# Static attention scores by half tiles: 64 queries times the 192 columns they need

## The chip, the core and the metric

The kernel runs on one core of a Trainium2 chip. TensorE multiplies matrices, VectorE, ScalarE and GpSimd work elementwise, SyncE issues most of the DMA transfers. The metric is the device time of one execution in microseconds. A run takes it several times; the medians are compared.

## What is computed

Four batches of eight heads, 768 positions of 64 numbers each, float32 throughout. A block-sparse attention is followed by a feed-forward layer:

```python
scores = (1.0 / np.sqrt(D)) * np.matmul(q, k.transpose(0, 1, 3, 2))
blk_i, blk_j = pos[:, None] // 32, pos[None, :] // 32
mask = np.abs(blk_i - blk_j) <= 1
mask = mask | (blk_i == 0) | (blk_j == 0) | (blk_i == 23) | (blk_j == 23)
for qb in range(24):
    for kb in sampled_blocks[qb]:                       # 3 per block
        mask[qb * 32:(qb + 1) * 32, kb * 32:(kb + 1) * 32] = True
scores = np.where(mask, scores, -1000000000.0)
...
attn = np.exp(scores - np.max(scores, axis=-1, keepdims=True))
attn = attn / (np.sum(attn, axis=-1, keepdims=True) + 1e-09)
x = attn @ v                                            # then [3072, 512]
h = x @ w_in                                            # 512 x 2048
out = (s * np.maximum(h, 0.0) ** 2 + b) @ w_out         # 2048 x 512
```

So a block of 32 queries sees its own block and the two neighbours, the first and the last block, and three sampled ones. The first and the last block of queries see all keys.

## The kernel before

**Order.** Attention comes first (0 to about 280 us), then the feed-forward layer, whose weights come as float64 and are taken apart into a high and a low part (the decode, lines 75 to 85) by VectorE and ScalarE, partly during attention. From about 546 us on the last two batches go through a scheme with seven products in place of eight (L1193).

**Slots.** The 22 middle blocks of queries are shifted by one block, so that a tile t of 128 queries holds four whole blocks. A static slot ("s") is one batch b, one tile t of 0 to 4 and one half x of the heads: 4 x 5 x 2 = 40 slots, each of four units, a unit being 128 queries of one head. Besides there are 8 slots "d" (the two blocks that see everything, 384 columns and two parts) and 4 slots "h" (the last half tile). 

**One static slot on TensorE**, in this order:

1. `transposes` (L787): the weights of a unit, 128 queries by 352 columns, are turned in three pieces of 128x128 by a product with a unit matrix, four units, 12 records. They go to one bank of PSUM per unit.
2. `x_transpose` (L858): two more for the slot before.
3. `scores_static` (L710), for the slot two further on: 128 queries times 256 columns (the tile's own 128 keys, the 64 keys of first and last block, the 64 keys behind the tile). Its contraction is 64 long, so the two heads of a pair use the upper and the lower rows of the array at the same time (`tile_position=(par * D, 0)`); each writes to a bank of its own. Four products.
4. `scores_sampled` (L736): the 96 sampled columns, per block of 32 queries.
5. `av_static` (L832): the turned weights times the values, two chunks of 128 keys for each half of 64 queries, which use the left and the right columns of the array.
6. `av_sampled` (L846): the same for the 96 sampled keys, per block of 32 queries.

A float32 product is two records in the trace, a transposition one. The mode of the array that a product uses is its tile size: 128x128, 64x128, 64x64, 64x32, 128x64 or 128x32 rows by columns. It follows from the shape of the operands or is given.

**The other engines.** VectorE takes the maximum of a unit, adding the mask `ms` (L751); ScalarE the exponential (L763); both take turns in copying the turned weights out of PSUM (L791, L793). In `ms` of 352 columns lie the window mask (built at L568 to L573) and the mask of sampled columns. Eight buffers `ptile` hold the weights, seven banks of PSUM go round for scores and transpositions, an eighth holds the value products.

**What sets the order.** TensorE's order in attention is a fixed line: the transpositions of slot i, the output transpositions of slot i - 1, the scores of slot i + 2, the value products of slot i. For the other engines a planner (`Plan`) simulates the program as it is built, with costs in ns that stand in the code (L956, L993, L1000, L1005), and writes the instructions of each engine in the order that it finds. Loads of k, q and v, the gathers and the decode of the weights are placed by the same planner.

**Keys and values.** `k_seq` holds per tile of keys 128 columns and then the 64 of first and last block, so that the 256 columns that a tile needs stand together, from 192 t on. `v_sta` holds the values of these 256 keys as two chunks of 128 rows: chunk 0 the tile's own keys, chunk 1 first and last block (rows 0 to 63) and the 64 keys behind (rows 64 to 127).

Of the kernel before, what the change touches and what calls it, by code (L numbers as in the profile page):

```python
# [9 lines left out]
F32 = mybir.dt.float32  # L10
# [192 lines left out]
def kernel(  # L203
# [27 lines left out]
    SC = 256  # L231
# [227 lines left out]
    with ExitStack() as es:  # L459
# [95 lines left out]
        def sampled_blocks():  # L555
# [146 lines left out]
        def scores_static(i, k):  # L702
# [4 lines left out]
            if kind == "s":  # L707
                for par in range(2):
                    sp = sps[(n + 2 * k + par, 0)] = next_bank(f"s{n + 2 * k + par}")
                    nc.tensor.matmul(sp[:, :SC], qr[halves[par], 2 * x + k, :], kt[halves[par], 2 * x + k, 192 * t:192 * t + SC],  # L710
                                     start=True, stop=True, tile_position=(par * D, 0))
                return
# [69 lines left out]

        def transposes(n, g):
            src = pbuf[(n, g)]
            tp = tps[(n, g)] = next_bank(f"t{n}_{g}")[:, :3 * P].rearrange("p (c q) -> p c q", c=3)
            for c in range(chunks(n)):
                nc.tensor.transpose(tp[:, c, :], src[:, c * P:(c + 1) * P], ident)  # L787
# [24 lines left out]
        def av_static(i, j):  # L812
# [17 lines left out]
            for c in range(2):  # L830
                for rows in halves:
                    nc.tensor.matmul(xs[rows], pt[:, c, rows], vt[:, c, hp * D:(hp + 1) * D], start=(j == 0 and c == 0),  # L832
                                     stop=False, skip_group_check=True)

        def av_sampled(i):
            kind, b, t, x = slots[i]
            n, vg = unit_of[i], vgs[(b, t)]
            for j in range(4):
                xs, pt = out_of(i, j), pts_of.pop(n + j)[0]
                for r in range(4):  # L840
                    rows = slice(r * BLK, (r + 1) * BLK)
                    if kind == "s":
                        w, m, h = pt[:NSL * BLK, 2, rows], r, 4 * x + 2 * (j % 2) + j // 2
                    else:
                        w, m, h = pt[:, 0, rows], r % 2, 4 * x + 2 * j + r // 2
                    nc.tensor.matmul(xs[rows], w, vg[:w.shape[0], m, h * D:(h + 1) * D], start=False, stop=(j == 3),  # L846
                                     tile_position=(0, r * BLK), skip_group_check=True)
# [108 lines left out]
        costs = {"s": (485, 535, 350, 260, 685), "d": (810, 0, 350, 780, 0), "h": (380, 535, 240, 160, 685)}  # L956
        cols = {"s": (1024, 1536, 768, 256, 1024), "d": (1536, 0, 768, 768, 0), "h": (640, 768, 512, 128, 512)}
        for i, (kind, b, t, x) in enumerate(slots):
# [31 lines left out]
            for j in range(nu):  # L990
                n, ms_ = u + j, []
                for g in range(ng):
                    o_m = op("v", {"s": 600, "d": 680, "h": 500}[kind], n + T["MP"], lambda n=n, g=g: maximum(n, g),  # L993
# [4 lines left out]
                for g in range(ng):  # L998
                    top = g == 0 and j == 0
                    o_e = op("a", {"s": 780, "d": 800, "h": 700}[kind], n + T["EP"], lambda n=n, g=g: exp(n, g), ms_,  # L1000
# [4 lines left out]
                    o_ev = op(on, {"a": 380, "v": 430}[on] if kind == "h" else {"a": 490, "v": 560}[on], n + T["EV"], lambda n=n, g=g, e=on: evacuate(n, g, e),  # L1005
# [378 lines left out]
```

## Time and profile before

| | |
|---|---|
| median of 3 runs | 813.33 us (811.89 to 817.2) |
| the profiled execution | 810.37 us, of it the span from first to last instruction 808.6 |
| granted clock of TensorE, mean | 0.992 |
| busy: TensorE, VectorE, ScalarE, GpSimd | 784.5, 559.1, 494.0, 214.7 us |
| TensorE's lines with most time, share of the chain that ended last | L1193 13%, L441, L442 and L440 10% each, L787 8%, L832 5%, L710 5% |

The span is what the profile shows; the executions' times are slightly longer. The last row comes from the chain of work that ended last: followed back from the last instruction, at each step to what released it. TensorE has 84% of that chain. Matmuls are pipelined, and a record lasts longer than the time until the next one starts; so what a stage costs is read from start to start and not from the duration of its records.

### The profile page before, as it was taken

Reading aid. Unit: us, or ns where it says so; the run is one execution under the profiler, and the core shown is the slowest. Engines: PE = TensorE matmul, PEld = TensorE weight load, DVE = VectorE, ACT = ScalarE, POOL = GpSimd, SP = SyncE. Lnnn points to the kernel's source line nnn. Section 1 sums busy time; section 2 is a strip of 40 time slices with the busy share of each in tenths; the row PEclk is TensorE's granted clock in tenths of the full one; section 3 lists DMA queues with packets and bytes.
Section 4 is the critical chain, followed back from the end, with each engine's and each line's share of the span. In section 5 each row is a group of like instructions: output and inputs, shape, how many; then the busy total and the mean of one; then the engine's idle time right before and its main releaser. Section 6 shows DMA issues by size and latency. Waiting matters only on the chain.

```text
span 808.6 us, 21993 instructions
## 1 busy us (share of the span) xinstructions
PE 784.5 (97%) x8400; PEld 682.2 (84%) x8400; DVE 559.1 (69%) x1379; ACT 494.0 (61%) x1175; POOL 214.7 (27%) x438
## 2 busy tenths in 40 slices
PE   7899999999998999999999999999999999999997
PEld 6687877888886889999889999998889988899996
DVE  5576778888887899999742222288768869766662
ACT  3576777878787787777663333457445457544542
POOL 5422133222400032222322222223223223322321
PEclk9899999999999999999999999999999999999999
DMA  9999897887777532433221010412200012000002
GB/s 267 248 223 315 231 253 215 244 246 215 220 210 235 144 107 83 130 127 105 86 98 40 27 40 27 150 52 79 86 1 7 0 40 85 16 0 1 1 2 78
DMA packets 86073, 95.61 MB, mean 118 GB/s; under 512 B 11344, under 2 KB 64976, under 8 KB 85968
## 3 DMA queue, kind: packets, MB, share of 16 engines
q1 hardware_dynamic: 85968, 94.21, 39.0%
q8 instruction: 66, 1.08, 0.6%
q14 instruction: 39, 0.32, 0.1%
HBM read 77.41 MB, written 12.58 MB: 111 GB/s over the span
## 4 chain that ended last, share of the span: by engine, by line
PE 84%; DMA 4%; ACT 4%; DVE 3%; issue 3%; SPq 2%; POOL 0%; ACTq 0%; DVEq 0%; POOLq 0%
PE m L1193 13%; PE o L441 10%; PE o L442 10%; PE o L440 10%; PE t L787 8%; PE xs L832 5%; PE s L710 5%; PE h L402 5%; PE h L403 5%; PE h L401 5%; PE xs L846 3%; PE s L736 2%; DMA kt<-in_k_seq_dram 2%; PE s L724 1%; PE xs L821 1%
## 5 line engine op out<-in xcount | busy, mean ns | idle before, releaser
L419 POOL TENSOR_TENSOR hid<-hid,hid 128x384 fp32r<-128x384 f32 x128 | 139.4, 1090 | 438.9 <-ACT hid L415 255.8
L763 ACT ACTIVATE ptile<-ptile,nm 128x352 f32<-128x352 f32 (+2 forms) x208 | 120.8, 584 | 30.5 <-DVE nm L751 29.5
L1210 ACT ACTIVATE hid<-hid,sb_b,sb_s 128x384 f32<-128x384 f32 x64 | 45.3, 708 | 111.9 <-DVE hid L1204 111.8
L410 DVE SCALAR_TENSOR_TENSOR hid<-hid,sb_s 128x384 f32<-128x384 f32 x64 | 40.9, 641 | 89.0 <-ACT hid L406 88.9
L670 POOL COPY kg<-kt 128x128 f32 x264 | 63.6, 294 | 134.9 <-PE s L736 123.9
L751 DVE CUSTOM_DVE_ANT_0 ptile<-s,ms 128x352 f32<-128x352 f32 x160 | 74.3, 521 | 27.8 <-PE s L736 27.5
L401 PE MATMUL h<-x,win 128*128 128x384 f32 x256 | 86.6, 338 | 0.6 <-ACT hid L406 0.6
L402 PE MATMUL h<-x,win 128*128 128x384 f32 x256 | 86.2, 337 | 0.2 <-DVE x L374 0.2
L403 PE MATMUL h<-x,win 128*128 128x384 f32 x256 | 86.4, 337 | 0.0
L787 PE MATMUL t<-ident,ptile 128*128 128x128 f32 x608 | 79.6, 280 | 6.4 <-ACT ptile L763 3.5
L787 PEld LDWEIGHTS t<-ident,ptile 128*128 128x128 f32 x608 | 66.3, 142 | 12.4 <-ACT ptile L763 4.3
L442 PE MATMUL o<-wout,hid 128*128 128x512 f32 x192 | 76.0, 396 | 0.0
L442 PE MATMUL o<-woutr,hid 128*128 128x512 f32 x192 | 76.0, 396 | 0.0
L441 PE MATMUL o<-wout,hid 128*128 128x512 f32 x192 | 75.9, 395 | 0.0
L441 PE MATMUL o<-woutr,hid 128*128 128x512 f32 x192 | 75.8, 395 | 0.0
L440 PE MATMUL o<-wout,hid 128*128 128x512 f32 x192 | 74.8, 389 | 0.0
L440 PE MATMUL o<-woutr,hid 128*128 128x512 f32 x192 | 74.7, 389 | 0.0
L406 ACT ACTIVATE hid<-h 128x384 f32<-128x384 f32 x64 | 31.2, 487 | 54.3 <-PE h L403 52.4
L791 DVE COPY pt<-t 128x384 f32<-128x384 f32 (+1 forms) x104 | 56.1, 545 | 9.9 <-PE t L787 8.0
L414 ACT ACTIVATE hid<-hid,sb_b 128x384 f32<-128x384 f32 x64 | 39.4, 615 | 37.2 <-DVE hid L410 37.2
L1193 PE MATMUL m<-xT,wop 128*128 128x384 f32 x288 | 58.5, 337 | 2.6 <-DVE sum L1286 1.5
L793 ACT COPY pt<-t 128x384 f32<-128x384 f32 (+1 forms) x104 | 48.8, 473 | 15.7 <-PE t L787 14.9
(169 smaller groups left out, 1648.8 us busy)
## 6 DMA issues: line engine op xcount, KB each, us to landing
vg<-in_v_dram SPq DMA_DIRECT2D x136, 128.0 KB, 3.9
v<-in_v_sta_dram SPq DMA_DIRECT2D x40, 256.0 KB, 4.5
kt<-in_k_seq_dram SPq DMA_DIRECT2D x16, 544.0 KB, 8.2
raw_i<-in_w_in_dram SPq DMA_DIRECT2D x16, 512.0 KB, 4.9
raw_o<-in_w_out_dram SPq DMA_DIRECT2D x16, 512.0 KB, 3.2
v<-in_v_dram SPq DMA_DIRECT2D x16, 384.0 KB, 5.4
xd<-xst SPq DMA_DIRECT2D x44, 128.0 KB, 3.9
out_dram<-ob SPq DMA_DIRECT2D x20, 256.0 KB, 2.2
```

The source lines that it names most:

```text
L401: nc.tensor.matmul(ph, wh, xh, start=(c == 0), stop=False)
L402: nc.tensor.matmul(ph, wh, xl, start=False, stop=False)
L403: nc.tensor.matmul(ph, wl, xh, start=False, stop=(c == NCC - 1))
L419: nc.gpsimd.tensor_tensor(out=htile(5 + i % 3), in0=t, in1=gh.bitcast(F32), op=ALU.subtract)
L440: nc.tensor.matmul(acc, gh[:, tsl], wout(f, 0), start=first, stop=False)
L441: nc.tensor.matmul(acc, gh[:, tsl], wout(f, 1), start=False, stop=False)
L442: nc.tensor.matmul(acc, gl[:, tsl], wout(f, 0), start=False, stop=last)
L670: nc.gpsimd.tensor_copy(kg[:, m], kts[b][:, :, bass.ds(box["js"][m], BLK)])
L751: nc.vector.tensor_tensor_reduce(out=pt[:, :w], in0=sps.pop((n, g))[:, :w], in1=msk, scale=-scale, scalar=FMAX if g == 0 else nm[:, 0:1], ...
L763: nc.scalar.activation(pt[:, :w], pt[:, :w], AF.Exp, bias=nms[n][:, last:last + 1], scale=-1.0, accum_out=dns[i][:, g, j:j + 1])
L787: nc.tensor.transpose(tp[:, c, :], src[:, c * P:(c + 1) * P], ident)
L1193: nc.tensor.matmul(to, w_, x_, start=(c == 0 and k == 0), stop=(c == 1 and k == 2))
```

## The change

Of the 256 static columns each half of a tile needs 192. The first 64 queries see the tile's own 128 keys and the 64 of first and last block (which stand ahead of the tile in `k_seq`, or behind it for t = 0), the other 64 the tile's second half, first and last block, and the 64 keys behind. The change lets each half compute its own 192 columns, with 64x64 tiles of the array, four at a time. A unit becomes 288 columns wide in place of 352.

The turned weights then are two full pieces of 128x128, and one piece that differs between the halves: 64 columns each, turned by an ordinary product with a 64x64 part of the unit matrix. The value products take a full chunk of 128 keys for each half, and a second product of 64 keys for each half. In `k_seq`, `v_sta` and the number of DMA transfers nothing changes. The mask is built to the new places, and the planner's costs are lowered.

```diff
-    SC = 256
+
+    SA = 64
+    SC = 192
     SW = SC + NSL * BLK
...
-        nc.gpsimd.memset(ms[:, :, P:P + 2 * BLK], 0.0)
-        nc.scalar.copy(ms[:, :, :P].rearrange("p t (c e) -> p t c e", e=BLK),
-                       wm[:, :4].unsqueeze(1).unsqueeze(3).broadcast_to([P, NSP, 4, BLK]))
-        nc.scalar.copy(ms[:, :, P + 2 * BLK:SC].rearrange("p t (c e) -> p t c e", e=BLK),
-                       wm[:, 4:].unsqueeze(1).unsqueeze(3).broadcast_to([P, NSP, 2, BLK]))
-        nc.gpsimd.memset(ms[:, 0, :BLK], NEG)
+        def window(rows, to, c, n):
+            nc.scalar.copy(ms[rows, :, to:to + n * BLK].rearrange("p t (c e) -> p t c e", e=BLK),
+                           wm[rows, c:c + n].unsqueeze(1).unsqueeze(3).broadcast_to([D, NSP, n, BLK]))
+
+        nc.gpsimd.memset(ms[:D, :, :SA], 0.0)
+        window(slice(0, D), SA, 0, 4)
+        window(slice(D, P), 0, 2, 2)
+        nc.gpsimd.memset(ms[D:, :, SA:2 * SA], 0.0)
+        window(slice(D, P), 2 * SA, 4, 2)
+        nc.gpsimd.memset(ms[:D, 0, SA:SA + BLK], NEG)
...
             if kind == "s":
+
+
+                places = [(0, SA, 192 * t, P), (0, 0, 192 * t + P, SA)] if t == 0 else [(0, 0, 192 * t - SA, SC)]
                 for par in range(2):
-                    sp = sps[(n + 2 * k + par, 0)] = next_bank(f"s{n + 2 * k + par}")
-                    nc.tensor.matmul(sp[:, :SC], qr[halves[par], 2 * x + k, :], kt[halves[par], 2 * x + k, 192 * t:192 * t + SC],
-                                     start=True, stop=True, tile_position=(par * D, 0))
+                    sps[(n + 2 * k + par, 0)] = next_bank(f"s{n + 2 * k + par}")
+                for a, to, o, w in places + [(1, 0, 192 * t + SA, SC)]:
+                    for par in range(2):
+                        nc.tensor.matmul(sps[(n + 2 * k + par, 0)][halves[a], to:to + w], qr[halves[par], 2 * x + k, halves[a]],
+                                         kt[halves[par], 2 * x + k, o:o + w], start=True, stop=True, tile_position=(par * D, a * D))
                 return
...
+        def tcols(n):
+            return 2 * P + D if slots[units[n][0]][0] == "s" else chunks(n) * P
+
         def transposes(n, g):
             src = pbuf[(n, g)]
-            tp = tps[(n, g)] = next_bank(f"t{n}_{g}")[:, :3 * P].rearrange("p (c q) -> p c q", c=3)
+            tp = tps[(n, g)] = next_bank(f"t{n}_{g}")[:, :tcols(n)]
+            if slots[units[n][0]][0] == "s":
+
+                for c in range(2):
+                    nc.tensor.transpose(tp[:, c * P:(c + 1) * P], src[:, SA + c * P:SA + (c + 1) * P], ident)
+                for h in halves:
+                    nc.tensor.matmul(tp[h, 2 * P:], src[h, :SA], ident[h, h], start=True, stop=True)
+                return
...
         def evacuate(n, g, eng):
-            o = ptp.tile([P, 3, P], F32, tag="pt", name=f"pt{n}_{g}")[:, :chunks(n)]
-            pts_of.setdefault(n, []).append(o)
-            copy_on(eng, o, tps.pop((n, g))[:, :chunks(n), :])
+            o = ptp.tile([P, 3 * P], F32, tag="pt", name=f"pt{n}_{g}")
+            pts_of.setdefault(n, []).append(o.rearrange("p (c q) -> p c q", c=3))
+            copy_on(eng, o[:, :tcols(n)], tps.pop((n, g)))
...
-            for c in range(2):
-                for rows in halves:
-                    nc.tensor.matmul(xs[rows], pt[:, c, rows], vt[:, c, hp * D:(hp + 1) * D], start=(j == 0 and c == 0),
-                                     stop=False, skip_group_check=True)
+            cols = slice(hp * D, (hp + 1) * D)
+            for a, rows in enumerate(halves):
+                nc.tensor.matmul(xs[rows], pt[:, 0, rows], vt[:, a, cols], start=(j == 0), stop=False, skip_group_check=True)
+            for a, rows in enumerate(halves):
+                nc.tensor.matmul(xs[rows], pt[rows, 2, :D], vt[rows, 1 - a, cols], start=False, stop=False,
+                                 tile_position=(a * D, a * D), skip_group_check=True)
...
-        costs = {"s": (485, 535, 350, 260, 685), "d": (810, 0, 350, 780, 0), "h": (380, 535, 240, 160, 685)}
+        costs = {"s": (390, 535, 350, 260, 685), "d": (810, 0, 350, 780, 0), "h": (380, 535, 240, 160, 685)}
```

The planner's other costs for static units fall too: the maximum from 600 to 540, the exponential from 780 to 725, the copies from 490 and 560 to 440 and 500 ns. The sampled value products read piece 1 of the turned weights where they read piece 2.

The first place is TensorE in the middle of attention, a static slot from its transpositions to the output transpositions. A row is a line, the operation, what it writes and what it reads, the shape written, and how often; `t` are the turned weights, `ptile` the weights, `xs` and `xss` the outputs. Before:

```order
L787 MATMUL t_0_1717<-ident,ptile_78 128x128 x3
L787 MATMUL t_0_1724<-ident,ptile_79 128x128 x3
L787 MATMUL t_0_1732<-ident,ptile_80 128x128 x3
L787 MATMUL t_0_1740<-ident,ptile_81 128x128 x3
L858 MATMUL xs_1643<-ident,xss_1736 128x128 x2
```

Now:

```order
L803 MATMUL t_0_1499<-ident,ptile_78 128x128 x2
L805 MATMUL t_0_1499<-ident,ptile_78 64x64 x2
L803 MATMUL t_0_1507<-ident,ptile_79 128x128 x2
L805 MATMUL t_0_1507<-ident,ptile_79 64x64 x2
L803 MATMUL t_0_1517<-ident,ptile_80 128x128 x2
L805 MATMUL t_0_1517<-ident,ptile_80 64x64 x2
L803 MATMUL t_0_1525<-ident,ptile_81 128x128 x2
L805 MATMUL t_0_1525<-ident,ptile_81 64x64 x2
L881 MATMUL xs_1424<-ident,xss_1514 128x128 x2
```

The third full transposition of each unit has become two products of 64x64, and these stand between the full ones of this unit and of the next.

The second place is TensorE further on in a slot, from the end of the sampled scores (`s` from the gathered keys `kg`) over the static value products (from the values `v` and the turned weights `pt`) to the sampled ones (from `vg`). Before:

```order
L736 MATMUL s_1766<-kg_2_861,qr_2s 32x96 x4
L832 MATMUL xs_1791<-v_0_1324,pt_0_1745 64x64 x4
L832 MATMUL xs_1791<-v_0_1324,pt_0_1751 64x64 x4
L832 MATMUL xs_1791<-v_0_1324,pt_0_1758 64x64 x4
L832 MATMUL xs_1791<-v_0_1324,pt_0_1768 64x64 x4
L846 MATMUL xs_1791<-vg_1_746,pt_0_1745 32x64 x4
```

Now:

```order
L747 MATMUL s_1399<-kg_1_558,qr_1s 32x96 x4
L853 MATMUL xs_1424<-v_0_944,pt_0_1374 64x64 x2
L855 MATMUL xs_1424<-v_0_944,pt_0_1374 64x64 x2
L853 MATMUL xs_1424<-v_0_944,pt_0_1381 64x64 x2
L855 MATMUL xs_1424<-v_0_944,pt_0_1381 64x64 x2
L853 MATMUL xs_1424<-v_0_944,pt_0_1385 64x64 x2
L855 MATMUL xs_1424<-v_0_944,pt_0_1385 64x64 x2
L853 MATMUL xs_1424<-v_0_944,pt_0_1393 64x64 x2
L855 MATMUL xs_1424<-v_0_944,pt_0_1393 64x64 x2
L869 MATMUL xs_1424<-vg_0_382,pt_0_1374 32x64 x4
```

All four products of a unit had the array shape 128x64 (the row shows what is written, 64x64). Now the two of L853 have it, and the two of L855 are 64x64 tiles, unit by unit in turn.

The third place is VectorE at the end of attention, from the last copy of turned weights (`pt`) to the first square of the feed-forward layer (`hid`). The rows with `wkhp`, `wklp` and `win` are decode steps of weights, `raw_i` the loaded float64, `x` the low part of the layer's input. Before:

```order
L791 COPY pt_0_6979<-t_0_6965 128x384
L85 SCALAR_TENSOR_TENSOR win_5480<-wklp_2709,wkhp_2700 128x512
L78 SCALAR_TENSOR_TENSOR wklp_2710<-wklp_2710,raw_i_6159 128x512
L83 TENSOR_TENSOR win_5480<-wkhp_2701,raw_i_6159 128x512
L84 TENSOR_SCALAR wkhp_2701<-win_5480 128x512
L852 TENSOR_TENSOR xss_7025<-xs_6992,rc_6975 128x128
L85 SCALAR_TENSOR_TENSOR win_5480<-wklp_2710,wkhp_2701 128x512
L75 TENSOR_SCALAR wkhp_2701<-raw_i_6271 128x512
L77 TENSOR_SCALAR wklp_2710<-raw_i_6271 128x512
L78 SCALAR_TENSOR_TENSOR wklp_2710<-wklp_2710,raw_i_6271 128x512
L410 SCALAR_TENSOR_TENSOR hid_7043<-hid_7043,sb_s 128x384
```

Now:

```order
L812 COPY pt_0_7323<-t_0_7309 128x384
L83 TENSOR_TENSOR win_6693<-wkhp_3131,raw_i_6466 128x512
L376 TENSOR_TENSOR x_1_7292<-wout_6625,x_0_6828 128x384 x2
L84 TENSOR_SCALAR wkhp_3131<-win_6693 128x512
L85 SCALAR_TENSOR_TENSOR win_6693<-wklp_3152,wkhp_3131 128x512
L875 TENSOR_TENSOR xss_7372<-xs_7335,rc_7319 128x128
L75 TENSOR_SCALAR wkhp_3132<-raw_i_6589 128x512
L77 TENSOR_SCALAR wklp_3153<-raw_i_6589 128x512
L78 SCALAR_TENSOR_TENSOR wklp_3153<-wklp_3153,raw_i_6589 128x512
L75 TENSOR_SCALAR wkhp_3132<-raw_i_6711 128x512
L412 SCALAR_TENSOR_TENSOR hid_7389<-hid_7389,sb_s 128x384
```

Eight decode steps stood between the two and seven do now, and the second low part of the input has moved in between. Ahead of this place, 37 rows of decode steps stood in VectorE's order, and 33 do now.

More of the change, by code (lines that the diff above doesn't have):

```diff
@@ L842, in av_sampled @@
                     if kind == "s":
-                        w, m, h = pt[:NSL * BLK, 2, rows], r, 4 * x + 2 * (j % 2) + j // 2
+                        w, m, h = pt[:NSL * BLK, 1, rows], r, 4 * x + 2 * (j % 2) + j // 2
                     else:
@@ L992 @@
                 for g in range(ng):
-                    o_m = op("v", {"s": 600, "d": 680, "h": 500}[kind], n + T["MP"], lambda n=n, g=g: maximum(n, g),
+                    o_m = op("v", {"s": 540, "d": 680, "h": 500}[kind], n + T["MP"], lambda n=n, g=g: maximum(n, g),
                              [*s_of[(n, g)], *([] if kind == "d" else [o_ss]), *ms_],
```

8 lines of the change are left out of this document (4 added, 4 removed).

## The prediction

> **What bounds the kernel now.** I read first the page's busy table, then the order of time on TensorE in the attention part, then who waits for whom, and the groups of VectorE and ScalarE last.
>
> ```profile
> PE 784.5 (97%) x8400; PEld 682.2 (84%) x8400; DVE 559.1 (69%) x1379; ACT 494.0 (61%) x1175; POOL 214.7 (27%) x438
> ```
>
> TensorE is busy for 97% of the span. That is an average, so the stage that changes has to be looked at alone. This is TensorE's order of time over one static slot (start, time to the last end, engine, line, operation, names, shape, records):
>
> ```profile
> 154.77 1.53 PE L787 MATMUL t<-ident,ptile 128*128 128x128 f32 x12
> 156.14 0.38 PE L858 MATMUL xs<-ident,xss 128*128 128x128 f32 x2
> 156.45 1.14 PE L710 MATMUL s<-kt,qr_0s 64*128 64x256 f32 x8
> 157.51 0.56 PE L736 MATMUL s<-kg,qr_0s 64*32 64x96 f32 x32
> 158.00 1.15 PE L832 MATMUL xs<-v,pt 128*64 128x64 f32 x32
> 159.09 0.65 PE L846 MATMUL xs<-vg,pt 96*32 96x64 f32 x32
> 159.67 0.55 PE L787 MATMUL t<-ident,ptile 128*128 128x128 f32 x3
> ```
>
> A stage lasts from its own start to the next one's: transposes 1.37 us, output transposes 0.31, static scores 1.06, sampled scores 0.49, static value products 1.09, sampled ones 0.58. The slot takes 159.67 - 154.77 = 4.90 us, and no row has an idle time in brackets. Here is a stretch of three such slots, busy us and counts in the order PE, PEld, DVE, ACT, POOL, then clock, DMA share and GB/s, and all waits of TensorE between 50 and 295 us (total, times, longest):
>
> ```profile
> 189.38:204.08 14.70, 14.70 (x361) 12.16 (x355) 12.26 (x43) 12.10 (x36) 4.24 (x18) 1.00 0.76 208
> ...
> PE xs L832 <- issue: 1.8, 2, 0.9
> PE t L787 <- issue: 1.5, 1, 1.5
> PE t L787 <- DVE nm L751: 1.4, 1, 1.4
> PE xs L858 <- DVE xss L852: 1.1, 1, 1.1
> PE xs L846 <- DMA vg<-in_v_dram: 0.9, 2, 0.6
> PE h L401 <- ACT hid L406: 0.6, 1, 0.6
> PE xs L821 <- ACT xst L863: 0.4, 1, 0.4
> ```
>
> TensorE fills 14.70 of 14.70 us, VectorE 12.26, ScalarE 12.10. All its waits of the attention part come to 7.7 us. So the 40 static slots are bound by TensorE, and what one slot gains or loses there is multiplied by 40.
>
> **What a change of array shape costs.** The change cuts columns, but it also lets TensorE alternate between array shapes inside a slot. So I need two prices apart: per record and per change of shape. The trace gives both wherever the same stage occurs in two sizes:
>
> ```profile
> 118.03 0.77 PE L724 MATMUL s<-kt,qr_5h 64*64 64x160 f32 x16
> 118.73 0.56 PE L736 MATMUL s<-kg,qr_5h 64*32 64x96 f32 x32
> ...
> 255.61 1.52 PE L724 MATMUL s<-kt,qr_5d 64*64 64x384 f32 x16
> 257.06 1.15 PE L832 MATMUL xs<-v,pt 128*64 128x64 f32 x32
> ...
> 123.77 1.15 PE L832 MATMUL xs<-v,pt 128*64 128x64 f32 x32
> 124.85 0.65 PE L846 MATMUL xs<-vg,pt 96*32 96x64 f32 x32
> 125.43 1.09 PE L787 MATMUL t<-ident,ptile 128*128 128x128 f32 x8
> 126.36 0.38 PE L858 MATMUL xs<-ident,xss 128*128 128x128 f32 x2
> 126.67 1.14 PE L710 MATMUL s<-kt,qr_4s 64*128 64x256 f32 x8
> ...
> 128.23 0.69 PE L826 MATMUL xs<-v,pt 128*64 128x64 f32 x16
> 128.84 0.65 PE L846 MATMUL xs<-vg,pt 128*32 128x64 f32 x32
> ```
>
> - 64x64 tiles, four at once: 16 records are 4 rounds. With 160 columns the stage takes 0.70 us, with 384 columns 1.45. The difference, 0.75 us over 4 x 224 columns, is 0.837 ns per column; 0.70 - 640 x 0.000837 leaves 0.16 us fixed.
> - 128x64, two at once: 32 records take 1.08 us, 16 take 0.61. That is 0.029 per record and 0.14 fixed.
> - 128x128: 14 records (154.77 to 156.45) take 1.68, 10 records (125.43 to 126.67) 1.24. That is 0.11 per record and 0.14 fixed.
>
> Three shapes, three times about the same fixed cost: 0.14 to 0.16 us for each run of one shape. A single crossing shows most of it:
>
> ```profile
> 156.25 0.27 PE L858 MATMUL xs<-ident,xss 128*128 128x128 f32 x1
> 156.45 0.49 PE L710 MATMUL s<-kt,qr_0s 64*128 64x256 f32 x2
> ```
>
> The last 128x128 record starts at 156.25, and the first of the other shape 0.20 later in place of 0.11. So 0.09 is the emptying of the array, and the other 0.05 to 0.07 the weights that can't be loaded ahead.
>
> The Trainium skill says the same without a price: in "TensorEngine Tiling (Array Packing)", section Key Properties, a change of tiling mode, unlike a change of tile, drains TensorE. "TensorE: Matmul & The Clock Gate", section Part 2, gives the drain as about 128 cycles, which at 2.4 GHz is 0.053 us, an estimate from that page; fifteen more changes a slot at that price would make about 830 us of the whole. The rows show 0.09 for the crossing alone and 0.14 to 0.16 in all, so I don't use it.
>
> **The change part by part, for one slot.**
>
> Transposes with output transposes, 1.68 us now. Afterwards: 8 + 2 full records x 0.11 = 1.10; the 128x128 shape is entered five times, 5 x 0.14 = 0.70; four small groups of 64x64 tiles, each 4 records in 2 rounds of 64 columns (2 x 64 x 0.837 ns = 0.107) and 0.16 fixed, 4 x 0.267 = 1.07. Together 2.87, so +1.19. One full transpose a unit goes (0.11), and its substitute costs as much in streaming alone.
>
> Static value products, 1.08 us now. Afterwards half the records stay 128x64: 4 groups of 4 x 0.029 + 0.14 = 0.26; the other half become four groups of 64x64 at 0.267. Together 2.10, so +1.02. There is no saving against it: two tiles ran at once before, and two do now.
>
> Static scores, 1.06 us now. Afterwards 16 records in 4 rounds of 192 columns: 0.16 + 4 x 192 x 0.000837 = 0.80, so -0.25. In the 8 slots with t = 0 the first half's keys come in two pieces, 128 and 64 columns one after the other on the same tiles, and the second half follows behind them: between 0.80 and 1.4, I take 1.16, so +0.10.
>
> That makes +1.96 in 32 slots and +2.31 in 8: 62.7 + 18.5 = **81 us** more on TensorE, 6.9 us a slot in place of 4.9.
>
> The narrower maxima, exponentials and copies (352 to 288 and 384 to 320 columns) save time on VectorE and ScalarE:
>
> ```profile
> L751 DVE CUSTOM_DVE_ANT_0 ptile<-s,ms 128x352 f32<-128x352 f32 x148 | 68.7, 521 | 24.8 <-PE s L736 24.5
> ...
> L751 DVE CUSTOM_DVE_ANT_0 ptile<-s,mh 128x256 f32<-128x256 f32 x16 | 5.8, 420 | 0.8 <-PE s L736 0.8
> ...
> L763 ACT ACTIVATE ptile<-ptile,nm 128x352 f32<-128x352 f32 x149 | 86.9, 586 | 12.3 <-DVE nm L751 11.5
> ```
>
> The maximum falls from 521 ns towards 420, at 288 columns about 454 by these two widths. I count nothing for it: this engine already waits for TensorE (24.5 us before this line alone), and now waits longer. The masks are built once, with one copy and one memset more; the first TensorE stage waits for the load of k anyway:
>
> ```profile
> 5.12 8.85 DMA kt<-in_k_seq_dram
> ```
>
> So that costs nothing either, and if the cover were gone, under 1 us.
>
> What comes back: of TensorE's 7.7 us of waits I take the first five rows, 6.7, as work of the DMA engines. One names a load; two wait for VectorE, which itself was held by a load of weights (the first row below); two have no releaser in the profile, and there the loads are only my reading, at a DMA share of 0.76 and more. The same bytes now have 80 us more, so I count 6.7 back (bounds 0 and 7.7).
>
> ```profile
> DVE wkhp L75 <- DMA raw_i<-in_w_in_dram: 4.0, 1, 4.0
> ...
> L78 DVE SCALAR_TENSOR_TENSOR wklp<-wklp,raw_i 128x512 f32<-128x512 int32 x7 | 4.7, 675 | 0.1
> ```
>
> At the start of the MLP about one decode less is done than before, since the planner believes the slots became shorter: 37 decode rows stood ahead of VectorE's last attention row, 33 do now. Such a row takes about 0.7 us (the second row above), four of them 2.7, and VectorE is nearly full afterwards:
>
> ```profile
> 300.00:350.00 50.00, 50.00 (x251) 45.11 (x250) 47.29 (x76) 39.01 (x70) 15.62 (x13) 1.00 0.35 110
> ```
>
> So between 0 and 3 us of new waiting, and I take 1. TensorE's own rate there doesn't change.
>
> Sum: the profiled execution took 810.4 us, 3 under the median of 813.3 and within the three runs' spread. 810.4 + 81.2 - 6.7 + 1 = **886 us**, 9% slower.
>
> **The rivals.**
>
> *The small groups don't run two at once.* Both 64x64 tiles of a pair use different rows of the array and write into one PSUM bank, on different partitions. No stage of before does that: at L724 and L736 tiles of different rows write to different banks, and the pairs of L832 that share a bank share the rows too. If they go one after the other, each of the 8 groups has 2 rounds more, 0.107 us: 8 x 0.107 x 40 = 34, so 920 us. In the Trainium skill, "TensorEngine Tiling (Array Packing)", Gotcha 1, says that different row tiles cannot use the same PSUM bank at the same time; no run here shows it. Against it stands that the partitions are disjoint. I give 0.08.
>
> *The clock falls.* TensorE loses half its clock after sparse stretches. The first two rows give TensorE alone (busy, clock, DMA share, GB/s), the third all engines:
>
> ```profile
> 24.15:27.56 3.41, 1.59 (x9) 1.00 1.11 242
> 27.56:30.97 3.41, 2.55 (x14) 0.50 1.06 244
> ...
> 246.01:249.42 3.41, 1.84 (x28) 1.30 (x16) 2.01 (x7) 1.21 (x4) 0.00 (x0) 1.00 1.07 378
> ```
>
> Weighted by the part of the array in use, the first stretch held 9 records of 64x64 x 768 / 4 = 1,700 column passes, and the next stretch ran at 0.50; the last held about 12 transposes x 256 = 3,070, and it stayed. The new slot's emptiest 3.41 us (both value stages and a little of the transposes) hold about 3,000: 1,536 + 768 + 700. That is close to what sufficed, and the average is 3,850. If it fell in one stretch per slot, the streaming there (a little over half of it) would take twice as long, 0.9 us x 40 = 37: 923 us. I give 0.07.
>
> *Only the emptying counts.* If the weights of the small groups can be loaded ahead, each change costs 0.09: some 0.9 us less a slot, 36 in all, so 850 us. Against it stand the three fixed costs above, which agree over all shapes. I give 0.06.
>
> *Not slower.* Suppose the fixed cost belongs to the change of line, of bank or of semaphore and not to that of shape. At a price p for each run of a shape the three stages change by 8 p - 0.01, 7 p - 0.04 and -0.25, together 15 p - 0.30, which decides at p = 0.02; at p = 0 the kernel takes 801 us. Against it: from L787 to L858 line and bank change, 12 records in 1.37 us run on at 0.11 each. I give 0.04. That TensorE's extra time hides under another engine is out, as it is the full one.
>
> **How the numbers follow.** Forecast 886 with 0.75; one after the other 920, 0.08; clock 923, 0.07; emptying only 850, 0.06; not slower 801, 0.04. The forecast's own spread: the fixed cost at 0.13 to 0.16 makes 15 x 0.015 x 40 = 9 us either way, what comes back 7, t = 0 some 2. The range 866 to 925 takes in the two slow rivals and leaves out the two fast ones. Faster or slower means by over 1%, about what a measurement here can tell: slower 0.96, the same 0.01, faster 0.03.
>
> **What would show it.** In TensorE's order of time, a static slot of 6.9 us; small groups of x4 between pairs of x2 transposes, 0.62 us from unit to unit; value products 0.52 us per unit; static scores 0.80. VectorE and ScalarE wait more for TensorE, the granted clock stays 1.00 after 50 us, and the MLP keeps its rate. If slots stay at 4.9 or fall below, the price of a change of shape is wrong; at 7.7 with even clock, the pairs run one after the other.

## The result

| | before | changed |
|---|---|---|
| median, 4 runs each | 814.79 us (811.89 to 817.2) | 883.68 us (881.37 to 891.3) |
| ratio of the changed to the one before | | 1.086, 95% interval 1.080 to 1.093 |
| the profiled execution, its span | 810.37, 808.6 us | 891.3, 889.5 us |
| granted clock of TensorE, mean | 0.992 | 0.985 |
| busy: TensorE, VectorE, ScalarE | 784.5, 559.1, 494.0 us | 867.7, 545.5, 481.5 us |

The kernel became 8.6% slower; 886 us had been forecast. The page's busy line shows the direction: TensorE gains 83 us, the two others lose about 13 each.

```profile
PE 867.7 (98%) x9264; PEld 712.0 (80%) x9264; DVE 545.5 (61%) x1379; ACT 481.5 (54%) x1176; POOL 215.0 (24%) x439
```

This is TensorE's order of time from one output transposition to the next, which is one static slot (start, time to the last end, engine, line, operation, names, shape, records):

```profile
131.15 0.44 PE L881 MATMUL xs<-ident,xss 128*128 128x128 f32 x2
131.52 0.88 PE L721 MATMUL s<-kt,qr_3s 64*64 64x192 f32 x16
132.33 0.56 PE L747 MATMUL s<-kg,qr_3s 64*32 64x96 f32 x32
132.82 0.34 PE L853 MATMUL xs<-v,pt 128*64 128x64 f32 x4
133.09 0.33 PE L855 MATMUL xs<-v,pt 64*64 64x64 f32 x4
133.35 0.34 PE L853 MATMUL xs<-v,pt 128*64 128x64 f32 x4
...
134.93 0.65 PE L869 MATMUL xs<-vg,pt 96*32 96x64 f32 x32
135.51 0.44 PE L803 MATMUL t<-ident,ptile 128*128 128x128 f32 x2
135.88 0.33 PE L805 MATMUL t<-ident,ptile 64*64 64x64 f32 x4
136.14 0.44 PE L803 MATMUL t<-ident,ptile 128*128 128x128 f32 x2
...
138.04 0.33 PE L881 MATMUL xs<-ident,xss 128*128 128x128 f32 x1
```

Read from start to start: static scores 0.81 us (1.06 before), static value products 134.93 - 132.82 = 2.11 (1.09 before), each unit 0.53 of it, and a unit of transpositions 0.63. The slot takes 138.04 - 131.15 = 6.89 us in place of 4.90, again without a row of idle time.

All waits of TensorE between 50 us and 395 us (total, times, longest), and the two groups of VectorE and the stretch of the MLP that answer to those shown of before:

```profile
PE o L443 <- DVE wout L85: 1.3, 2, 0.7
PE xs L842 <- ACT xst L886: 0.4, 1, 0.4
...
L762 DVE CUSTOM_DVE_ANT_0 ptile<-s,ms 128x288 f32<-128x288 f32 x152 | 60.5, 454 | 40.9 <-PE s L747 40.8
L812 DVE COPY pt<-t 128x320 f32<-128x320 f32 x78 | 38.4, 492 | 37.8 <-PE t L805 37.7
...
400.00:450.00 50.00, 50.00 (x253) 45.33 (x252) 47.65 (x78) 38.06 (x70) 13.96 (x13) 1.00 0.32 106
```

Of 7.7 us of waits 1.7 are left. VectorE's maximum fell from 521 to 454 ns, and VectorE waits all the longer for TensorE: 40.8 us before this line where there were 24.5.

One thing stands out early: half a clock for 20 us. The rows below the first are stretches of TensorE (from and to, length, busy, records, clock, DMA share, GB/s); the first row is its longest wait in the first 50 us, just ahead of the half clock:

```profile
PE xs L842 <- DMA v<-in_v_dram: 3.5, 1, 3.5
...
40.31:43.73 3.42, 0.28 (x10) 1.00 1.16 201
43.73:64.21 20.48, 20.14 (x255) 0.50 0.60 169
105.17:108.58 3.41, 3.41 (x88) 1.00 0.69 218
```

This explains why the profiled execution is the slowest of its kernel. At half clock a stretch counts as half its length in the mean clock, so span x (1 - clock) estimates what the clock cost: time minus span x (1 - clock) is 891.3 - 13.3 = 878.0 for it, 881.37 - 3.5 = 877.9 for the fastest and 883.95 - 5.3 = 878.7 for one in the middle. So most of the difference between the runs of the changed kernel is how long the clock was at half.

### The profile page after: what moved, and what is told of

Its sections match the earlier page's. It is cut to its first block, busy times and chain, and to the rows that moved or that the text cites. A ratio compares the mean times of both kernels' runs of the same rounds, so it can differ in the third digit from the quotient of the medians.

```text
span 889.5 us, 23735 instructions
## 1 busy us (share of the span) xinstructions
PE 867.7 (98%) x9264; PEld 712.0 (80%) x9264; DVE 545.5 (61%) x1379; ACT 481.5 (54%) x1176; POOL 215.0 (24%) x439
## 4 chain that ended last, share of the span: by engine, by line
PE 86%; DVE 5%; DMA 4%; ACT 3%; issue 1%; SPq 1%; ACTq 0%; DVEq 0%
PE m L1216 12%; PE o L443 9%; PE o L444 9%; PE o L442 9%; PE t L803 7%; PE xs L853 5%; PE t L805 5%; PE xs L855 5%; PE h L404 4%; PE h L405 4%; PE h L403 4%; PE s L721 4%; PE xs L869 3%; PE s L747 2%; DMA kt<-in_k_seq_dram 2%; PE xs L881 2%
## 5 line engine op out<-in xcount | busy, mean ns | idle before, releaser
L774 ACT ACTIVATE ptile<-ptile,nm 128x288 f32<-128x288 f32 (+2 forms) x208 | 112.4, 542 | 30.2 <-DVE nm L762 29.9
L814 ACT COPY pt<-t 128x320 f32<-128x320 f32 (+2 forms) x104 | 44.4, 432 | 96.6 <-PE t L805 90.3
L762 DVE CUSTOM_DVE_ANT_0 ptile<-s,ms 128x288 f32<-128x288 f32 x160 | 63.6, 454 | 42.3 <-PE s L747 42.1
L812 DVE COPY pt<-t 128x320 f32<-128x320 f32 (+2 forms) x104 | 51.5, 495 | 42.6 <-PE t L805 40.0
L803 PE MATMUL t<-ident,ptile 128*128 128x128 f32 x320 | 72.2, 308 | 0.0
L1216 PE MATMUL m<-win 128*128 128x384 f32 x288 | 55.9, 338 | 0.0
```

Source lines behind the costliest of these rows:

```text
L762: nc.vector.tensor_tensor_reduce(out=pt[:, :w], in0=sps.pop((n, g))[:, :w], in1=msk, scale=-scale, scalar=FMAX if g == 0 else nm[:, 0:1], ...
L774: nc.scalar.activation(pt[:, :w], pt[:, :w], AF.Exp, bias=nms[n][:, last:last + 1], scale=-1.0, accum_out=dns[i][:, g, j:j + 1])
L803: nc.tensor.transpose(tp[:, c * P:(c + 1) * P], src[:, SA + c * P:SA + (c + 1) * P], ident)
L1216: nc.tensor.matmul(to, w_, x_, start=(c == 0 and k == 0), stop=(c == 1 and k == 2))
```

## Experiments

The theory is the prediction's: each run of products of one array shape costs TensorE about 0.15 us beyond its streaming, and the change makes 20 such runs out of 5 per slot. Against it stand that the small products are dear in themselves or run one at a time, and that the narrower scores bring nothing.

**Only the value products as in the change, in the kernel before.**

```diff
-            for c in range(2):
-                for rows in halves:
-                    nc.tensor.matmul(xs[rows], pt[:, c, rows], vt[:, c, hp * D:(hp + 1) * D], start=(j == 0 and c == 0),
-                                     stop=False, skip_group_check=True)
+            cols = slice(hp * D, (hp + 1) * D)
+            for a, rows in enumerate(halves):
+                nc.tensor.matmul(xs[rows], pt[:, a, rows], vt[:, a, cols], start=(j == 0), stop=False, skip_group_check=True)
+            for a, rows in enumerate(halves):
+                nc.tensor.matmul(xs[rows], pt[rows, 1 - a, rows], vt[rows, 1 - a, cols], start=False, stop=False,
+                                 tile_position=(a * D, a * D), skip_group_check=True)
```

> The kernel before with the static value products alone as the change has them: for each unit two products of 128 keys (128x64 tiles) and two of 64 keys (64x64 tiles). Columns, mask, scores and transpositions stay. The keys left out have weight zero. If a run of one shape costs about 0.15 us: eight runs in place of one, value products 2.1 us in place of 1.09, slot 5.9, 40 us more, 855 us. If alternating costs nothing: as many rounds as before, slot 4.9, 815 us. If the pairs of 64x64 tiles that share a bank run one after the other: 0.4 us a slot beyond the 2.1.

Measured: 841.9 us, ratio 1.038 (1.034 to 1.043). TensorE's order of time in one slot:

```profile
88.48 0.34 PE L832 MATMUL xs<-v,pt 128*64 128x64 f32 x4
88.75 0.33 PE L834 MATMUL xs<-v,pt 64*64 64x64 f32 x4
...
90.59 0.66 PE L848 MATMUL xs<-vg,pt 96*32 96x64 f32 x32
91.18 1.53 PE L787 MATMUL t<-ident,ptile 128*128 128x128 f32 x12
...
97.10 1.53 PE L787 MATMUL t<-ident,ptile 128*128 128x128 f32 x12
```

The value products take 90.59 - 88.48 = 2.11 us and the slot 97.10 - 91.18 = 5.92, as the theory has it, with no column fewer or more than before. The total rose by 32 us (profiled spans 840.6 and 808.6), not by the 40 that were expected: the slots cost 40 x 1.02 = 41, but the waits fell from 7.7 to 1.0 us, and the time lost to the clock by 1.5 (0.008 x 808.6 against 0.006 x 840.6). Like the change itself, a slower TensorE gets its waits back.

**The changed kernel with its products regrouped.** `av_grouped` puts the four units' small value products behind the four units' full ones; `t_grouped` does so with the transpositions, and the copies out of PSUM then wait for the slot's last small one; `both_grouped` does both.

```diff
-            for a, rows in enumerate(halves):
-                nc.tensor.matmul(xs[rows], pt[rows, 2, :D], vt[rows, 1 - a, cols], start=False, stop=False,
-                                 tile_position=(a * D, a * D), skip_group_check=True)
+            if j < 3:
+                return
+            for jj in range(4):
+                hp, pt, xs = 2 * (jj % 2) + jj // 2, pts_of[n + jj][0], out_of(i, jj)
+                cols = slice(hp * D, (hp + 1) * D)
+                for a, rows in enumerate(halves):
+                    nc.tensor.matmul(xs[rows], pt[rows, 2, :D], vt[rows, 1 - a, cols], start=False, stop=False,
+                                     tile_position=(a * D, a * D), skip_group_check=True)
...
-                for h in halves:
-                    nc.tensor.matmul(tp[h, 2 * P:], src[h, :SA], ident[h, h], start=True, stop=True)
+                if units[n][1] < 3:
+                    return
+                for m in range(n - 3, n + 1):
+                    for h in halves:
+                        nc.tensor.matmul(tps[(m, g)][h, 2 * P:], pbuf[(m, g)][h, :SA], ident[h, h], start=True, stop=True)
...
```

> The changed kernel with only the value products regrouped: the four units' 128x64 products, then the four units' 64x64 ones. Two runs of a shape in place of eight. If a run costs 0.147 us: value products 2.07 us to 1.2, slot 6.0, 35 us less, 848 us. If the products are dear in themselves: no change, 884 us.

> The changed kernel with only the transpositions regrouped: the four units' full ones, then the small ones. Three runs of a shape in place of nine (the output transpositions are the third). If a run costs 0.147 us: 2.86 us to 2.0, slot 6.0, 35 us less, 848 us, unless the later copies hold up the scores for want of a bank; then TensorE waits for VectorE or ScalarE there. If the products are dear in themselves: no change, 884 us.

> The changed kernel with the same products in another order: all full transpositions of a slot's four units, then all small ones; all 128x64 value products, then all 64x64 ones. The copies out of PSUM wait for the small transpositions. Runs of one shape in a slot: 8 in place of 20. If a run costs 0.147 us: 12 x 0.147 = 1.76 us less, slot 5.1 in place of 6.88, 71 us less, about 813 us. If the small products themselves are dear (or the number of records): slot 6.9, 884 us. If late copies or too few banks hold up TensorE in exchange: between the two, with waits of TensorE for VectorE or ScalarE before the scores.

| | runs of one shape per slot | slot, us | median, us | ratio to before |
|---|---|---|---|---|
| changed | 20 | 6.89 | 883.68 | 1.086 (1.080 to 1.093) |
| av_grouped | 14 | 6.01 | 855.06 | 1.051 (1.040 to 1.062) |
| t_grouped | 14 | 6.00 | 848.50 | 1.043 (1.031 to 1.054) |
| both_grouped | 8 | 5.12 | 825.32 | 1.017 (1.013 to 1.021) |

The same products, in the same number, and only their order differs: six runs fewer take 0.88 us off the slot, twelve 1.77. That is 0.147 us for each run, in both places. The medians of `av_grouped` and `t_grouped` are of two executions each, those of the others of four. The slots of `av_grouped` (first two rows) and `t_grouped`, from transpositions to transpositions:

```profile
88.38 0.44 PE L803 MATMUL t<-ident,ptile 128*128 128x128 f32 x2
...
94.39 0.44 PE L803 MATMUL t<-ident,ptile 128*128 128x128 f32 x2
...
93.01 1.09 PE L803 MATMUL t<-ident,ptile 128*128 128x128 f32 x8
...
99.01 1.09 PE L803 MATMUL t<-ident,ptile 128*128 128x128 f32 x8
```

One slot of `both_grouped` on TensorE:

```profile
93.79 1.09 PE L803 MATMUL t<-ident,ptile 128*128 128x128 f32 x8
94.81 0.68 PE L808 MATMUL t<-ident,ptile 64*64 64x64 f32 x16
95.43 0.44 PE L889 MATMUL xs<-ident,xss 128*128 128x128 f32 x2
95.79 0.88 PE L721 MATMUL s<-kt,qr_2s 64*64 64x192 f32 x16
96.60 0.56 PE L747 MATMUL s<-kg,qr_2s 64*32 64x96 f32 x32
97.09 0.69 PE L856 MATMUL xs<-v,pt 128*64 128x64 f32 x16
97.71 0.68 PE L863 MATMUL xs<-v,pt 64*64 64x64 f32 x16
98.32 0.65 PE L877 MATMUL xs<-vg,pt 96*32 96x64 f32 x32
```

Sixteen records of 64x64 take 0.61 us (97.71 to 98.32), as long as sixteen of 128x64 (0.62). So the pairs of small tiles run two at once although they share a bank.

The totals follow the slots less and less: 71 us were expected for both, 58 came. In `both_grouped` TensorE's waits in attention are back at 10.9 us (1.7 in the changed kernel), the longest of them for the gathered values `vg`. That accounts for the total: 71 us of slots less 9.2 of waits are 62, and the profiled spans differ by 61.0 (889.5 and 828.5). For 7.6 of the 10.9 us the profile names no releaser, so whether later copies and fewer free banks, as the expectation feared, hold TensorE up there stays open.

**Only the scores by half tiles, in the kernel before.** The remaining part of the change, in the layout of 256 columns. It needs the banks of PSUM to be kept as tiles, which `banks_kept` alone does.

```diff
-                    sp = sps[(n + 2 * k + par, 0)] = next_bank(f"s{n + 2 * k + par}")
-                    nc.tensor.matmul(sp[:, :SC], qr[halves[par], 2 * x + k, :], kt[halves[par], 2 * x + k, 192 * t:192 * t + SC],
-                                     start=True, stop=True, tile_position=(par * D, 0))
+                    sps[(n + 2 * k + par, 0)] = next_bank(f"s{n + 2 * k + par}")
+                for a in range(2):
+                    for par in range(2):
+                        nc.tensor.matmul(sps[(n + 2 * k + par, 0)][halves[a], a * D:a * D + 192], qr[halves[par], 2 * x + k, halves[a]],
+                                         kt[halves[par], 2 * x + k, 192 * t + a * D:192 * t + a * D + 192], start=True, stop=True,
+                                         tile_position=(par * D, a * D))
...
-            return bank(bcount[0] % NBANK, name)
+            k = bcount[0] % NBANK
+            if k not in banks:
+                banks[k] = bank(k, f"b{k}")
+            return banks[k]
```

> The kernel before with the static scores alone by half tiles: the 256-column layout, the mask, the transpositions and the value products stay as they were. The 64 columns that a half does not need keep what its bank of PSUM held, and the mask takes them out. Shapes alternate no more often than before. If a column costs 0.837 ns on a tile and each run of one shape about 0.15 us: static scores 0.80 us in place of 1.06, slot 4.65 in place of 4.90, 40 x 0.25 = 10 us less, ratio to before 0.988. If 64x64 tiles are dear in themselves: the scores at 1.06 or more, ratio 1.00 or above. If VectorE or the loads become the bound once TensorE is faster: the scores at 0.80, but the slot near 4.9 with new waits, ratio 1.00.

> The kernel before, whose seven banks of PSUM are seven tiles kept all along in place of a new tile for each use; nothing else. It is the base that scores_only needs. All theories: ratio 1.00 within 0.01, slot 4.90.

Measured: `banks_kept` 0.9994 (0.997 to 1.002), `scores_only` 1.002 (1.000 to 1.004). TensorE's slot is as short as expected, 94.49 - 89.84 = 4.65 us with scores of 0.81:

```profile
89.84 1.53 PE L795 MATMUL b<-ident,ptile 128*128 128x128 f32 x12
91.21 0.38 PE L866 MATMUL xs<-ident,xss 128*128 128x128 f32 x2
91.52 0.88 PE L717 MATMUL b<-kt,qr_2s 64*64 64x192 f32 x16
92.33 0.56 PE L744 MATMUL b<-kg,qr_2s 64*32 64x96 f32 x32
...
94.49 1.53 PE L795 MATMUL b<-ident,ptile 128*128 128x128 f32 x12
```

But the 10 us did not reach the end. The waits of TensorE between 50 and 290 us:

```profile
PE xs L854 <- DMA vg<-in_v_dram: 6.5, 5, 2.3
PE xs L866 <- DVE xss L860: 2.3, 3, 1.1
PE b L795 <- DVE nm L759: 2.0, 1, 2.0
...
```

The last output transposition of attention starts at 286.3 us, 5 us later than before (281.3, and 279.3 with `banks_kept`), although each slot is 0.25 us shorter. Between 40 and 260 us, 17 us ran at half clock, in three pieces, where the kernel before had none there. So two things eat the gain: waits, and the clock that falls behind them. The clock's part shows in every execution: the mean granted clock of the 12 runs of `scores_only` was 0.9865, that of the 23 of the kernel before 0.992, which over a span of 810 us is 4.7 us more lost; with span x (1 - clock) taken off, `scores_only` is some 2.5 us faster and not slower.

**Where that gain went.** First the order: the planner is told the new costs (`scores_planned`), and besides a slower rate of loads (`scores_bw`).

```diff
-        costs = {"s": (485, 535, 350, 260, 685), "d": (810, 0, 350, 780, 0), "h": (380, 535, 240, 160, 685)}
-        cols = {"s": (1024, 1536, 768, 256, 1024), "d": (1536, 0, 768, 768, 0), "h": (640, 768, 512, 128, 512)}
+        costs = {"s": (390, 535, 350, 260, 685), "d": (810, 0, 350, 780, 0), "h": (380, 535, 240, 160, 685)}
+        cols = {"s": (768, 1536, 768, 256, 1024), "d": (1536, 0, 768, 768, 0), "h": (640, 768, 512, 128, 512)}
...
-                dma = max(dma, o.end + 650.0) + o.nbytes / 280.0
+                dma = max(dma, o.end + 650.0) + o.nbytes / 230.0
```

> scores_only, with the planner told the new cost of the static scores (390 in place of 485 ns, 768 in place of 1024 columns). The slots of scores_only had fallen to 4.65 us, but its waits in attention had risen from 7.7 to 13.1 us, most for the gathered values. If these waits come from an order that was planned for slower slots: fewer waits, ratio to before 0.985 to 0.995. If the loads can't come faster: waits as in scores_only, ratio 1.00.

> scores_planned, with the planner's rate for loads at 230 in place of 280 bytes per ns, near the 200 to 240 GB/s that the trace shows in attention: loads of weights are planned farther apart. If the waits come from weights that push ahead of gathered values and keys: fewer waits, ratio 0.985 to 0.995. If the loads of attention alone are the limit: ratio 1.00; if the weights now come too late for the feed-forward layer: above 1.00, with waits of TensorE for decode steps.

Measured: 1.012 (1.008 to 1.016) and 1.010 (1.006 to 1.013). The first fits neither of its cases; the second fits its last one, weights that come too late for the feed-forward layer. Attention ends earlier than with `scores_only`, the last output transposition starts at 279.2 and 278.8 us, but at the head of the feed-forward layer TensorE now waits for VectorE's decode steps. This is the row of `scores_bw` between 275 and 450 us:

```profile
PE o L440 <- DVE wout L83: 6.9, 1, 6.9
```

With `scores_planned` it is 2.6 us, and both have 6.8 us at half clock there. Then the loads of feed-forward weights, held back until attention's last value products, with the kernel before and with `scores_only`:

```diff
-            pw = op("s", 450, N + T["WP"] - 4 + T["WS"] * k, load, [prev_k], alloc=[raw], nbytes=524e3, late=T["LATE"])
+            pw = op("s", 450, N + T["WP"] - 4 + T["WS"] * k, load, [prev_k, o_av], alloc=[raw], nbytes=524e3, late=T["LATE"])
```

> The kernel before with all loads of feed-forward weights held back until the last value products of attention; the decode then lies wholly behind attention, and the total is much longer. Only attention's end is compared: 277 us in the kernel before. If its waits in attention come from the loads of weights: slots of 4.90 without the longer ones, attention's end some 5 us earlier. If the gathered values are late in themselves: the same waits for vg.

> scores_only with the loads of weights held back in the same way. If the loads of weights take the gain away: attention ends 10 us earlier than in late_before (40 x 0.25 us). If the gathered values themselves are the limit: waits for vg as in scores_only, and attention ends less than 5 us earlier.

Measured, by the start of the last output transposition: 278.9 and 273.4 us. So with no weights under way the narrower scores end attention 5.5 us earlier, where with them they ended it 5 us later. That is between the two theories. Of the 15 us that separate a loss of 5 from the expected gain of 10, holding the weights back returns 10.5. Part of that is the clock: from 10 us to attention's end 23.9 us ran at half clock in `scores_only` and 10.2 in the kernel before, and about the same in the two late versions (13.7 each). The rest stays lost, with waits for `vg` of 4.0 us in `late_scores` and 2.1 in `late_before`. These are single executions, `banks_kept` alone moved attention's end by 2 us, and which load is late by what other one was not followed up. None of the versions tried is faster than the kernel before.

**The clock.** One artificial wait in slot 32, in both kernels: GpSimd fills a small tile 24 times, and one more product of TensorE, to a bank that nobody reads, needs that tile.

```diff
+        def hold_up(n):
+            nc.gpsimd.tensor_copy(hold_t[:, :P], pbuf[(n, 0)][:, :P])
+            for _ in range(24):
+                nc.gpsimd.memset(hold_t, 1.0)
+
+        def let_go():
+            nc.tensor.matmul(next_bank("hold")[:, :P], ident, hold_t[:, :P], start=True, stop=True)
...
+            if i == 32:
+                line.append(held)
```

> The kernel before with one artificial wait: in slot 32 TensorE waits for a chain of 24 memsets on GpSimd, about 5 us, through one more product. If the clock depends on the array's work per 3.41 us and the old slot is dense enough at half clock: the clock falls for one or two stretches (3.4 to 6.8 us) and recovers, so the wait plus 2 to 3.5 us. If a wait of 5 us leaves the clock alone: 1.00 throughout, the wait alone.

> The changed kernel with the same artificial wait in slot 32. If the emptier slot at half clock (2,000 to 2,700 weighted columns per stretch in the profiled execution) is too sparse to bring the clock back at once: half clock for some 10 to 20 us after the wait, slots of 10 to 11 us, 5 to 10 us lost beyond the wait. If what was seen between 43 and 64 us belongs to the start of the kernel: recovery after one or two stretches, as in the kernel before.

TensorE's wait and the stretches behind it, in `hold_before`:

```profile
PE hold L796 <- POOL hold_t L793: 4.7, 1, 4.7
...
183.83:187.25 3.42, 0.25 (x3) 1.00 0.91 245
187.25:194.07 6.82, 5.29 (x74) 0.50 0.65 184
194.07:197.49 3.42, 3.42 (x60) 1.00 0.22 77
```

And in `hold_after`:

```profile
PE hold L817 <- POOL hold_t L814: 1.7, 1, 1.7
...
232.44:235.85 3.41, 2.20 (x20) 1.00 0.71 223
235.85:263.16 27.31, 26.81 (x338) 0.50 0.33 97
```

The old slots leave half clock within 6.8 us, the changed ones after 27.3 us, and that although the wait was much shorter, 1.7 against 4.7 us. The totals, of one execution each, are 812.4 us (the kernel before took 810.7 to 817.3 beside it; TensorE's other waits fell from 7.7 to 4.6 us) and 895.3 us (883.7 without the wait). So the changed kernel stays at half clock for so long in the middle of attention too, and the early 20 us of the profiled execution need no other cause than the wait ahead of them.

## Why the prediction was right

**The price of a run of one shape** was taken as 0.14 to 0.16 us from three stages in two sizes, and regrouping shows it directly: 0.147. This is the step that carries the result. It was argued from stages of before; `av_only` and the regrouped kernels show that it is the alternation, since the same products in fewer runs cost accordingly less. How the 0.147 us divides into the emptying of the array and weights that are not loaded ahead, as the prediction has it, no run separates.

**The three stages.** Transpositions with output transpositions: 6.89 - 0.81 - 0.49 - 2.11 - 0.58 = 2.90 us (2.87 in the sum). Value products 2.11 (2.10). Static scores 0.81 (0.80). The slot is 6.89 us where 6.9 was written.

**The slots with t = 0** are the one term that was sized wrongly. They were put at 1.16 us of scores, between 0.80 and 1.4:

```profile
186.99 0.94 PE L721 MATMUL s<-kt,qr_0s 64*64 64x128 f32 x24
187.86 0.56 PE L747 MATMUL s<-kg,qr_0s 64*32 64x96 f32 x32
```

They take 0.87, close to the lower bound. Eight such slots make the sum 2.3 us too high, less than the rest of it is uncertain by.

**What comes back** was 6.7 of 7.7 us, with 1 us of new waits at the start of the MLP; measured are 6.0 less (1.7 left, with 1.3 of them new, for VectorE's decode). That loads stood behind the waits without a named releaser was my reading, and no run shows it. That longer slots have fewer waits holds in the main but not strictly: 10.9 us at slots of 5.12 (`both_grouped`), 7.7 at 4.90 (before), 1.0 at 5.92 (`av_only`), 0.5 at 6.00 (`t_grouped`), 4.2 at 6.01 (`av_grouped`).

**The sum.** 32 x 1.99 + 8 x 2.04 = 80.0 us on TensorE, -6.0 of waits, which include the new ones, and 6.8 more lost to the clock (13.3 against 6.5): 810.4 + 80.8 = 891.2 for the profiled execution, which took 891.3. That it closes to 0.1 us is luck. The waits of the first 50 us, which it leaves out, rose from 8.4 to 11.8 us, and half a clock costs less than half of its stretch: in the changed kernel a slot with t = 0 takes 11.4 us there (50.07 to 61.45 us) and not twice 6.94. With the estimated cost of the clock taken off both, the rise is 878.0 - 803.9 = 74.1 us, where the forecast had 81.2 - 6.7 + 1 = 75.5. That 886 came so near the median of 883.7 is partly luck too: the forecast set out from an execution 4.4 us under the median of before, and the medians lie 68.9 us apart. The median lies under the profiled execution because in the other runs the clock fell for a shorter time.

**The rivals.** That the small groups run one after the other is refuted: four records take 0.26 us with the change of shape, as four in two rounds should. The Trainium skill ("TensorEngine Tiling (Array Packing)", Gotcha 1) would have different row tiles keep out of one bank; here two of them write to disjoint partitions of one bank at the same time, without loss. That only the emptying counts is refuted by 0.147. That the change of shape is free is refuted by the regrouping; nor is it the bank that costs, since in `t_grouped` the four units' banks are gone through twice in a slot where they were once, and the time falls. The falling clock came true in part: not in every slot, as that rival had it, but once for 20 us, set off by a wait. After the half clock, a stretch at full clock held about 2,950 weighted column passes at its lowest (105.17 to 108.58 us), and the clock stayed; the forecast's 3,000 was right for that.

**What was not seen** is how little the -0.25 us of the scores is worth by itself. The prediction's branch "not slower" put it at 801 us; `scores_only` made just this slot and came out at 1.002. The forecast didn't rest on it, as it went the other way.

## What to carry to other kernels

Before splitting products into smaller tiles, count the runs of one array shape on TensorE as well as the columns: here 64 columns fewer in four matmul rounds gained 0.25 us a slot, and fifteen more runs cost 2.2. The same products sorted by shape got back 1.77 us of it. And where the waits of an engine are few but hang on loads, time taken off that engine can come back as waits, and these can cost it the clock as well; a gain there has to be checked by the end of the stage, not by its slot.

## What the runs showed of the hardware

TensorE's clock has a memory in this kernel. I cut TensorE's records at stretches of 3.41 us, the steps in which the clock changes, and counted each record's column passes where it starts: two for each column of a float32 record, times the share of the 128x128 array that its tile covers. At full clock, stretches of 2,950 kept it and one of 2,180 (the wait in `hold_after`) lost it. The other traces agree: of all fourteen, from 35 us to the end of attention, the 18 stretches after which the clock fell held at most about 2,300 passes, and the 1,037 after which it stayed at least about 2,770. Idle time alone doesn't decide it: in the kernel before, the stretch from 246.01 us, busy for only 1.84 us but with about 3,070 passes, kept the clock, and the one of `hold_after`, busy for 2.20 us, lost it.

At half clock, stretches of 1,580 to 2,820 stayed there and those of 2,850 and 3,070 ended it (the changed kernel and `hold_after`). In `scores_only` one of 2,940 stayed, so near 2,900 this count can't tell. The changed slot, 7,680 passes, makes on average some 3,800 per stretch at full clock but only about 2,300 at half, where it takes 11.3 us (in `hold_after`) in place of 6.9: so it keeps a full clock and hardly regains a lost one. The old slot, 9,216 passes in 4.90 us, makes some 6,400 and regained the clock within two stretches.

The Trainium skill ("TensorE: Matmul & The Clock Gate", section Why this matters for your kernels) warns of idle gaps above about 3 us. Here a wait of 1.7 us was enough, because the work around it was sparse.
